# Sliding-window attention with routed experts: the first three routed blocks by seven products, their weight sums on GpSimd, routing dealt out behind every product

## The chip, the cores and the metric

The kernel runs on one core of a Trainium2 chip. The metric is device time in microseconds (us) of one execution, as the median over several runs. Of one execution there is also a hardware profile. In the profile TensorE is PE (its weight loads PEld), VectorE DVE, ScalarE ACT, GpSimd POOL and SyncE SP.

## The reference, cut to what matters

Causal attention with a window of 64 over (8, 8, 576, 64) gives 4608 rows x of 512 numbers. Each row goes through one of 8 experts, all in fp32:

```python
e = argmax(x @ w_gate)          # or the expert of the row before, where x @ w_local says so
p = softmax(x @ w_gate)[e]
out[row] = p * (relu(x[row] @ w1[e]) @ w2[e])   # w1[e]: 512 x 1024, w2[e]: 1024 x 512
```

The expert of a row is taken over from the row before it when a sigmoid gate is at least 0.5, so the choice runs along each sequence of 576 rows as a scan.

## The kernel before

The program has two phases that overlap at their border. **Attention** works through nine groups of 512 rows. Behind it, **routing** finds each row's expert, counts the rows of every expert, and writes tables that say which rows make up each block, with what weight p, and with which expert. It has two halves: the first (`Router.first`) covers the first three sequences and runs within attention; the second (`Router.second`) covers the other rows and runs beside the first three expert blocks. Both are Python generators: after each piece of work they yield the time in us that VectorE is thought to need for it, and whether TensorE's next piece has to wait for it. In `second` the pieces are `gate` (logits to expert, with small transposes on TensorE in between: L801 for vk, L811, L821, L833, and the counting products L845 and L846), then the arithmetic on eight counts per expert, then the places `pl` of the rows (128x296), then `table`: for four pieces of up to ten chunks it builds one-hot matrices `rowh`, `one` and `colh` on VectorE (L934, L939, L944), and TensorE adds up their products (L951). At the end the indices `gx` and `idx` and the weights `pw` are there, and the later blocks' rows can be fetched.

**Experts** work on blocks of 256 rows of one expert (and a few of 128 and 64). The first three, numbered -1, -2 and -3, come from routing's first half (`FB = 3`); thirteen big ones follow, with eight small ones between. A block is `fetch` (two gathers of 128 rows on GpSimd's queue, and two transfers of 2 MB for w1 and w2 on SP's), `turn` (eight transposes on TensorE, two copies into `xt`), `hidden` (relu(x @ w1)) and `result` (h @ w2, times p, with a scatter of each half on GpSimd's queue). Weights land in a ring of four buffers, so w1 of block n+2 is asked for when block n's w1 has been read.

A block is computed in one of two ways. *Plain* (L1275, L1307) uses 32 and 16 full matmuls. *Fast* is the scheme that multiplies 2x2 quarters with seven products in place of eight. It needs sums of the quarters: four of `xt` (128x256 each, tile xs), four of w1 (128x1024, tile ws1), four of w2 (128x1024, ws2) and four of h (128x512, hs). `left` and `right` write them, `prepare` calls those for xt and w1, and `big_hidden` and `big_result` (products at L1184 and L1227 of the kernel before) the others. Each of the sum tiles has one buffer. Between products ScalarE keeps copies of what a PSUM accumulator holds so far, and VectorE adds such a copy to another accumulator (L1195 for h, L1236 for y). Three accumulators px, py and pz are used by turns, so the last product of a half has to wait until the addition that reads px is done.

Blocks -1 and -2 are plain before the change (`PLAIN = (-1, -2)`), block -3 and all later big blocks are fast. While routing's second half runs, only TensorE's order is written out by hand (`manual_schedule(engines={ET.PE})`), and a planner orders VectorE, ScalarE and GpSimd. From block -3 on VectorE and ScalarE are in program order too. TensorE's pieces of routing are dealt out by `step()`, after each group of a plain hidden half and twice per half of a result; each call lowers a pause by `STEP = 3.5`, and a piece is given out when the pause has run down. The whole second half is done before the hidden half of block -3.

Of the kernel before, what the change touches and what calls it, by code (L numbers as in the profile page):

```python
# [8 lines left out]
F32 = mybir.dt.float32  # L9
# [6 lines left out]
ET = mybir.EngineType  # L16
# [3 lines left out]
P = 128  # L20
# [49 lines left out]
MID = (KB, KB - 1)  # L70
PLAIN = (-1, -2)

# [90 lines left out]
def attention(ctx, tc, ring, kq, v3, v4, vt, vh, xs, lt, ok, wg, wg2, ident, rt, ex):  # L163
# [125 lines left out]
    build_mask(0)  # L289
    allr = cp.tile([P, NSC, HP, 2, 4], F32, name="allr")  # L290

# [400 lines left out]
class Router:  # L692
# [306 lines left out]
    def second(self, psum):  # L999
# [16 lines left out]
        rest = tl("rest", P, E)  # L1016
        vec.tensor_tensor(rest, cnt, lim, op=Alu.subtract)
        ns = tl("ns", P, E)
        self.shifted(ns, rest, HF - 1, P.bit_length() - 1)
# [21 lines left out]
        vec.tensor_tensor(steph, hoff, send, op=Alu.subtract)  # L1041
        vec.tensor_scalar(steph, steph, float(P), float((HF0 - SM0) * P), Alu.mult, Alu.add)
        CE = [P, CV, E]
        pl, none = tl("pl", *CE), tl("none", P, C1, E)
# [3 lines left out]
        vec.tensor_tensor(pl, pl, mid(off).to_broadcast(CE), op=Alu.add)  # L1048
        yield 6.0, False
        plh = tl("plh", *CE)  # L1050
# [4 lines left out]
        vec.tensor_tensor(pl[:, :C1], pl[:, :C1], none, op=Alu.add)  # L1055
        vec.tensor_tensor(pl, pl, self.oh, op=Alu.mult)
        lo, hi = self.places(pl, CV)
        ej = tabs["ej"]
        self.experts_of(ej[:, :NBLK], NBLK, [(NB, bend), (E, send), (E, hend)])
# [3 lines left out]
        vec.scalar_tensor_tensor(ej[:, NBLK:], bend[0:1, E - 1:], float(SURE[0]), more, Alu.is_gt, Alu.max)  # L1063
        yield 6.0, False
        at = yield from self.table(psum, slice(0, CV), NS, lo, hi, tabs["idx"], tabs["pw"], tabs["gx"])
# [12 lines left out]
class Experts:  # L1078
# [12 lines left out]
    def rows(self, st, n):  # L1091
        tabs = self.tabs
        if n < 0:
            idx, pw, gx, rows = tabs["idx1"], tabs["pw1"], tabs["gx1"], ZR + 1
            slots = range(-2 - 2 * n, -2 * n)
        else:
            idx, pw, gx, rows = tabs["idx"], tabs["pw"], tabs["gx"], N + 2
            slots = range(2 * n, 2 * n + 2) if n < NB else range(SM0 + n - NB, SM0 + n - NB + 1)
        st.update(x=[], slots=slots, idx=idx, pw=pw, rows=P, big=len(slots) == 2, fast=len(slots) == 2 and n not in PLAIN)
        if n >= NB + E:  # L1100
            st.update(half=n - NB - E, rows=HF)
        for s in slots:
            x = (self.xp if n == -1 else self.xq).tile([P, D], F32, name="xg")
            self.nc.gpsimd.indirect_dma_start(  # L1104
                out=x, out_offset=None, in_=self.xs[:rows, :],
                in_offset=bass.IndirectOffsetOnAxis(ap=gx[:, s:s + 1], axis=0))
            st["x"].append(x)
        return st
# [14 lines left out]
    def turn(self, st, quiet):  # L1123
        nc, n = self.nc, st["rows"]
        st["xt"] = xt = self.xtp.tile([P, DK, BIG], F32, name="xt")
        for i, x in enumerate(st["x"]):
            tp = self.ps_t.tile([P, DK, P], F32, name="tp")
            for kk in range(DK):
                nc.tensor.transpose(tp[:, kk, :n], x[:n, kk * P:(kk + 1) * P], self.ident[:n, :n])  # L1129
            (nc.scalar.copy if quiet else nc.vector.tensor_copy)(xt[:, :, i * P:i * P + n], tp[:, :, :n])  # L1130
        if st["fast"] and not quiet:
            self.prepare(st)

    def prepare(self, st):

        st["xq"] = quarters(st["xt"], DK, BIG)
        st["xt"] = self.right("xs", st["xq"])
        w = quarters(st["w1"], DK, F)

        st["wq"] = [[w[0][0], w[1][0]], [w[0][1], w[1][1]]]  # L1140
        st["ws"] = self.left("ws1", st["wq"])

    def left(self, name, a):

        sub, add = Alu.subtract, Alu.add
        s1, s2, s3, s4 = self.sums(name, a)
        for o, x, y, op in ((s1, a[1][0], a[1][1], add), (s2, s1, a[0][0], sub), (s3, a[0][0], a[1][0], sub),
                            (s4, a[0][1], s2, sub)):
            self.nc.vector.tensor_tensor(o, x, y, op=op)
        return s1, s2, s3, s4  # L1150

    def right(self, name, b):

        sub = Alu.subtract
        t1, t2, t3, t4 = self.sums(name, b)
        for o, x, y in ((t1, b[0][1], b[0][0]), (t2, b[1][1], t1), (t3, b[1][1], b[0][1]), (t4, b[1][0], t2)):
            self.nc.vector.tensor_tensor(o, x, y, op=sub)
        return t1, t2, t3, t4
# [4 lines left out]

    def big_hidden(self, st):

# [7 lines left out]
        st["w2q"] = w2 = quarters(st["w2"], FK, D)  # L1173
        st["w2t"] = self.right("ws2", w2)
        st["h"] = h = self.wk.tile([P, FK, BIG], F32, name="h", bufs=1)
# [22 lines left out]
        product(px, a[0][0], b[0][0], stop=False)  # L1198
        u = keep(0, px)
        product(py, s[0], t[0], stop=False)  # L1200
        z = keep(1, py)
        product(px, s[1], t[1], False, False)
        v = keep(2, px)
        product(pz, a[0][1], b[1][0])
        relu(hq[0][0], pz, u)
        product(px, s[2], t[2], False, False)
        relu(hq[1][1], px, z)
        product(py, s[3], b[1][1], False)
        relu(hq[0][1], py, v)
        product(px, a[1][1], t[3], False)  # L1210
        relu(hq[1][0], px)

        st["ha"] = [[hq[0][0], hq[1][0]], [hq[0][1], hq[1][1]]]
        st["hs"] = self.left("hs", st["ha"])

    def big_result(self, st):

# [20 lines left out]
        product(px, a[0][0], b[0][0], stop=False)  # L1238
        u = keep(0, px, pw[0])
        product(py, s[0], t[0], stop=False)  # L1240
        z = keep(1, py, pw[1])
        product(px, s[1], t[1], False, False)
        v = keep(2, px, pw[0])
        product(pz, a[0][1], b[1][0])
        put(0, 0, pz, u)
        product(px, s[2], t[2], False, False)
        put(1, 1, px, z)
        product(py, s[3], b[1][1], False)
        put(0, 1, py, v)
        self.scatter(st, 0, y[0])  # L1250
        product(px, a[1][1], t[3], False)
        nc.scalar.activation(y[1][:, :w], px, Act.Copy, scale=pw[1])
        self.scatter(st, 1, y[1])

    def scatter(self, st, i, y):
# [5 lines left out]
    def hidden(self, st, quiet, step):  # L1261
        nc = self.nc
        if st["fast"]:
            return self.big_hidden(st)
        n = BIG if st["big"] else st["rows"]
# [17 lines left out]

    def result(self, st, step):
        nc = self.nc
        if st["fast"]:
            return self.big_result(st)
        if "half" in st:
# [27 lines left out]
    def space(self, ctx):  # L1316
        tc = self.tc
        self.xtp = ctx.enter_context(tc.tile_pool(name="ex_xt", bufs=2))
        self.xq = ctx.enter_context(tc.tile_pool(name="ex_xq", bufs=6))
        self.wk = ctx.enter_context(tc.tile_pool(name="ex_work", bufs=2))  # L1320
        self.one = ctx.enter_context(tc.tile_pool(name="ex_one", bufs=1))
        self.ps_t = ctx.enter_context(tc.tile_pool(name="ex_ps_t", bufs=2, space=PSUM))
# [3 lines left out]
    def run(self, ctx, rt, last=None):  # L1326
# [3 lines left out]
        ps_r = ctx.enter_context(tc.tile_pool(name="ex_ps_r", bufs=1, space=PSUM))  # L1330
        ctx.enter_context(tc.manual_schedule(engines={ET.PE}))
        rt.rows_of(ctx, tc, "rt_oh2")
# [5 lines left out]
        side = rt.second(psum)  # L1338
        pause = 0.0

        def step():
            nonlocal side, pause
            pause -= STEP
            if pause > 0.0:
                return
            pause, trip = 0.6, False
            while side and not trip:
                w, trip = next(side, (0.0, None))
# [8 lines left out]
        for n in range(SURE[0]):  # L1357
            order.append(n)
            if n % 2 and between:
                order.append(between.pop(0))  # L1360
        order += between + half[:1]
        jobs += [self.fetch(n) for n in order[1:FB]]
        self.turn(jobs[0], True)
        step()
        for i, n in enumerate(order):
            quiet = i < FB
            if i == FB - 1:
                while side:
                    step()
                if last:  # L1370
                    last(psum())

                ctx.enter_context(tc.manual_schedule(engines={ET.PE, ET.DVE, ET.Activation}))
                jobs.append(self.fetch(order[FB]))
                if jobs[i]["fast"]:
                    self.prepare(jobs[i])
            if i + 2 > FB and i + 2 < len(order):
                jobs.append(self.fetch(order[i + 2]))
            self.hidden(jobs[i], quiet, step)
            if i + 1 < len(order):  # L1380
# [60 lines left out]
```

## Time and profile before

| what | us |
|---|---|
| three runs: median (lowest to highest) | 657.9 (657.87 to 658.69) |
| the profiled execution's own time | 659.1 |
| its span, first to last instruction | 657.1 |
| attention's last matmuls end | 136.4 |
| block -1, hidden half begins (first L1275) | 136.4 |
| block -3, hidden half begins (first L1184) | 202.4 |
| fourth block, hidden half begins | 228.6 |

The span of 657.1 us leaves 2.0 us around it. A row of the timeline has the start in us from the span's start, the duration in us, engine, line, operation, tiles out and in with shapes (partitions x elements), and in brackets the idle time before it with what ended it. A row of a table by stretches has each engine's busy us and its number of instructions (x), the granted TensorE clock as a share of the full one, the share of time that the DMA engines were busy, and GB/s.

### The profile page before, as it was taken

The numbers are of one execution on the slowest core, as the hardware profiler recorded it, in microseconds if no ns is written. First come the engines' busy times: TensorE is split into PE (matmuls) and PEld (weight loads), VectorE is DVE, ScalarE is ACT, GpSimd is POOL, SyncE is SP. The second block draws the span as 40 slices with busy tenths as digits, with TensorE's granted clock in tenths as the row PEclk, the third lists the DMA queues.
The fourth block names the chain that finished last, engine by engine and source line by source line (L and its number), as shares of the span: only waits on it lengthen the run. The fifth ranks groups of instructions, "written<-read, shape, count | busy, mean of one in ns | idle before, by whom it ended". The sixth has DMA issues, their size and how long they took to land. (4 is left out here: it accounts for less than half of the span.)

```text
span 657.1 us, 14909 instructions
## 1 busy us (share of the span) xinstructions
PE 629.8 (96%) x6431; PEld 544.8 (83%) x6431; DVE 401.2 (61%) x723; ACT 181.8 (28%) x314; POOL 125.8 (19%) x131
## 2 busy tenths in 40 slices
PE   7888988899999999999999999999999999999995
PEld 7777767675757999889989998999799979997974
DVE  6675589665984866378628835852765276527310
ACT  4756655421111232112212121221122112211200
POOL 4322122220014111121104113211311130101011
PEclk9999998899999999999999999999999999999999
DMA  8999999895436555595578748746864685457540
GB/s 337 415 346 360 351 377 355 327 378 199 161 144 241 195 212 218 173 397 204 184 278 315 269 180 314 289 169 215 305 240 165 221 309 219 161 213 283 193 157 23
DMA packets 22032, 165.80 MB, mean 252 GB/s; under 512 B 3485, under 2 KB 4515, under 8 KB 11972
## 3 DMA queue, kind: packets, MB, share of 16 engines
q1 hardware_dynamic: 13108, 135.24, 55.4%
q0 software_dynamic: 8848, 29.50, 11.3%
q8 instruction: 53, 0.87, 0.5%
q14 instruction: 23, 0.19, 0.1%
HBM read 145.85 MB, written 19.40 MB: 251 GB/s over the span
## 5 line engine op out<-in xcount | busy, mean ns | idle before, releaser
L1257 POOL DMA_INDIRECT out_dram<-y,idx x36 | 40.9, 1136 | 335.6 <-DVE y L1236 149.2
L1184 PE MATMUL hp<-xs,ws 128*128 128x128 f32 x672 | 79.6, 275 | 0.0
L1184 PEld LDWEIGHTS hp<-xs,ws 128*128 128x128 f32 x672 | 77.3, 192 | 0.0
L1227 PE MATMUL hp<-ws,hs 128*128 128x256 f32 x336 | 77.1, 379 | 0.0
L1275 PE MATMUL hp<-xt,w 128*64 128x64 f32 (+2 forms) x896 | 74.1, 260 | 0.0
L1275 PEld LDWEIGHTS hp<-xt,w 128*64 128x64 f32 (+1 forms) x896 | 68.6, 161 | 5.8 <-issue 2.4
L1227 PEld LDWEIGHTS hp<-ws,hs 128*128 128x128 f32 x336 | 63.8, 190 | 8.7
L1195 DVE TENSOR_TENSOR h<-hp,keep 128x512 f32<-128x512 f32 x42 | 28.8, 690 | 57.3 <-PE hp L1184 57.3
L1104 POOL DMA_INDIRECT xg<-xs,gx x40 | 45.7, 1144 | 72.7 <-PE tp L1129 58.9
L1307 PE MATMUL yp<-w,h 128*128 128x512 f32 x128 | 56.4, 593 | 0.0
L1184 PEld LDWEIGHTS hp<-xt,w 128*128 128x128 f32 x448 | 53.0, 192 | 2.9 <-issue 1.9
L1184 PE MATMUL hp<-xt,w 128*128 128x128 f32 x448 | 54.9, 276 | 0.0
L1236 DVE SCALAR_TENSOR_TENSOR y<-hp,pw,kept 128x256 f32<-128x256 f32 x42 | 19.7, 480 | 57.1 <-issue 33.3
L1227 PE MATMUL hp<-w,h 128*128 128x256 f32 x224 | 53.3, 381 | 0.0
L416 DVE TENSOR_TENSOR p<-p,mask 128x1024 f32<-128x1024 f32 x31 | 38.6, 1244 | 20.6 <-ACT p L411 20.5
L380 PEld LDWEIGHTS sp<-w 64*64 64x64 f32 x1296 | 37.6, 134 | 16.3 <-issue 13.1
L411 ACT ACTIVATE p<-sp 128x512 f32<-128x512 f32 x72 | 39.3, 596 | 40.1 <-PE sp L380 37.9
L426 PE MATMUL xo<-va,p 128*64 128x74 f32 (+1 forms) x576 | 45.7, 233 | 3.3 <-DVE va L343 3.3
L426 PE MATMUL xo<-vb,p 128*64 128x74 f32 (+1 forms) x576 | 45.7, 233 | 3.2 <-ACT p L300 1.5
L380 PE MATMUL sp<-w 64*64 64x128 f32 (+1 forms) x1296 | 43.3, 265 | 5.5 <-issue 4.7
L426 PEld LDWEIGHTS xo<-vb,p 128*64 128x64 f32 x576 | 39.9, 141 | 7.9 <-issue 4.7
L1307 PEld LDWEIGHTS yp<-w,h 128*128 128x128 f32 x128 | 23.7, 190 | 26.9 <-issue 26.1
(257 smaller groups left out, 945.9 us busy)
## 6 DMA issues: line engine op xcount, KB each, us to landing
w<-in_w_dram SPq DMA_DIRECT2D x48, 2048.0 KB, 9.0
w<-in_kq_dram SPq DMA_DIRECT2D x17, 1024.0 KB, 9.4
xs<-x POOLq DMA_DIRECT2D x9, 1024.0 KB
va<-in_v_dram SPq DMA_DIRECT2D x5, 1184.0 KB
vtt<-in_vt_dram SPq DMA_DIRECT2D x5, 1024.0 KB
va<-in_v_dram SPq DMA_DIRECT2D x3, 1040.0 KB, 9.0
va<-in_v_dram SPq DMA_DIRECT2D x2, 520.0 KB, 6.6
w<-in_kq_dram SPq DMA_DIRECT2D x2, 512.0 KB
```

Source lines behind the costliest of these rows:

```text
L380: nc.tensor.matmul(sp[j][c * WIN:(c + 1) * WIN, a:b], lhsT=kt[h, hp, block * WIN:(block + 1) * WIN], rhs=qt[h, hp, a:b], start=not biased, ...
L411: nc.scalar.activation(p[:, j], sp[j], Act.Exp, scale=DH ** -0.5)
L416: masked.append(nc.vector.tensor_tensor(p, p, m.to_broadcast([P, 2, SC]), op=Alu.mult))
L426: nc.tensor.matmul(xo[par * WIN:(par + 1) * WIN, j, s * VW:s * VW + n], lhsT=p[:, j, b * WIN:(b + 1) * WIN], rhs=w[:, s, 2 * hp + j, :n], ...
L1104: self.nc.gpsimd.indirect_dma_start(out=x, out_offset=None, in_=self.xs[:rows, :], in_offset=bass.IndirectOffsetOnAxis(ap=gx[:, s:s + 1], ...
L1184: nc.tensor.matmul(out[:, m, :], lhsT=a[:, kk, m * P:(m + 1) * P], rhs=b[:, kk, :], start=start and m + kk == 0, stop=stop and (m, kk) == ...
L1195: nc.vector.tensor_tensor(o, x, y, op=add)
L1227: nc.tensor.matmul(out, lhsT=a[:, m, :], rhs=b[:, m, :], start=start and m == 0, stop=stop and m == FK // 2 - 1, skip_group_check=True)
L1236: nc.vector.scalar_tensor_tensor(y[i][:, j * w:(j + 1) * w], x, pw[i], y2, Alu.mult, Alu.add)
L1257: self.nc.gpsimd.indirect_dma_start(out=self.out[:, :], out_offset=bass.IndirectOffsetOnAxis(ap=st["idx"][:, s:s + 1], axis=0), in_=y, in_ ...
L1275: nc.tensor.matmul(hp[a, i, :], lhsT=st["w1"][:, kk, m * P:(m + 1) * P][:, a], rhs=st["xt"][:, kk, :n], start=(kk == 0), stop=(kk == DK - 1))
L1307: nc.tensor.matmul(yp, lhsT=st["h"][:, m, i * P:(i + 1) * P], rhs=st["w2"][:, m, :], start=(m == 0), stop=(m == FK - 1))
```

## The change

Blocks -1 and -2 become fast too (`PLAIN` goes, `fast` holds for every big block). For the three early blocks GpSimd writes the sums of w1, and for blocks -1 and -2 also those of w2; the rest stays on VectorE. The copies of xt for the early blocks stay on ScalarE. `step()` is now called after each of the seven products of a half, it lowers the pause by `QUIET = 1.25`, and routing's second half yields in smaller pieces; it may run until the end of block -3's hidden half. While it runs, TensorE, VectorE, ScalarE and GpSimd are all in program order. The flag for the rare path and the fetches of the fourth and fifth block follow after block -3's hidden half, and the fourth block's `turn` is called from inside block -3's result, after four of its seven products. The pool of the sum tiles is opened ahead of the gathered rows' pool, and `allr` moves to another pool.

```diff
-PLAIN = (-1, -2)
+QUIET = 1.25
...
-    allr = cp.tile([P, NSC, HP, 2, 4], F32, name="allr")
+    allr = wk.tile([P, NSC, HP, 2, 4], F32, name="allr", bufs=1)
...
         vec.tensor_tensor(pl, pl, mid(off).to_broadcast(CE), op=Alu.add)
-        yield 6.0, False
+        yield 1.9, False
...
-        if st["fast"] and not quiet:
+        if st["fast"]:
             self.prepare(st)
...
-        st["ws"] = self.left("ws1", st["wq"])
+        st["ws"] = self.left("ws1", st["wq"], self.nc.gpsimd if st["early"] else self.nc.vector)
...
-        st["w2t"] = self.right("ws2", w2)
+        st["w2t"] = self.right("ws2", w2, nc.gpsimd if -FB < st["early"] < 0 else nc.vector)
...
         product(px, a[0][0], b[0][0], stop=False)
         u = keep(0, px)
+        step()
         product(py, s[0], t[0], stop=False)
...
         product(pz, a[0][1], b[1][0])
         put(0, 0, pz, u)
+        step()
+        mid()
         product(px, s[2], t[2], False, False)
         put(1, 1, px, z)
+        step()
...
-        ctx.enter_context(tc.manual_schedule(engines={ET.PE}))
+        early = ExitStack()
+        early.enter_context(tc.manual_schedule(engines={ET.PE, ET.DVE, ET.Activation, ET.Pool}))
...
-        pause = 0.0
+        pause, room = 0.0, QUIET
...
-            pause -= STEP
+            pause -= room
...
-            pause, trip = 0.6, False
-            while side and not trip:
+            trip = False
+            while side and not trip and pause <= 0.0:
...
+        def rest():
+            early.close()
+            ctx.enter_context(tc.manual_schedule(engines={ET.PE, ET.DVE, ET.Activation}))
+            if last:
+                last(psum())
+            jobs.extend(self.fetch(n) for n in order[FB:FB + 2])
+        self.turn(jobs[0], True)
         jobs += [self.fetch(n) for n in order[1:FB]]
         for i, n in enumerate(order):
+            if i + 2 >= FB + 2 and i + 2 < len(order):
+                jobs.append(self.fetch(order[i + 2]))
+            self.hidden(jobs[i], i < FB, step)
             if i == FB - 1:
                 while side:
                     step()
+                rest()
+                self.result(jobs[i], step, lambda: self.turn(jobs[FB], False))
+                continue
```

More of the change, by code (lines that the diff above doesn't have):

```diff
@@ L1017, in second @@
         vec.tensor_tensor(rest, cnt, lim, op=Alu.subtract)
+        yield 1.6, False
         ns = tl("ns", P, E)
@@ L1042, in second @@
         vec.tensor_scalar(steph, steph, float(P), float((HF0 - SM0) * P), Alu.mult, Alu.add)
+        yield 1.6, False
         CE = [P, CV, E]
@@ L1056, in second @@
         vec.tensor_tensor(pl, pl, self.oh, op=Alu.mult)
+        yield 2.4, False
         lo, hi = self.places(pl, CV)
+        yield 2.2, False
         ej = tabs["ej"]
@@ L1063, in second @@
         vec.scalar_tensor_tensor(ej[:, NBLK:], bend[0:1, E - 1:], float(SURE[0]), more, Alu.is_gt, Alu.max)
-        yield 6.0, False
+        yield 1.2, False
         at = yield from self.table(psum, slice(0, CV), NS, lo, hi, tabs["idx"], tabs["pw"], tabs["gx"])
@@ L1098, in rows @@
             slots = range(2 * n, 2 * n + 2) if n < NB else range(SM0 + n - NB, SM0 + n - NB + 1)
-        st.update(x=[], slots=slots, idx=idx, pw=pw, rows=P, big=len(slots) == 2, fast=len(slots) == 2 and n not in PLAIN)
+        st.update(x=[], slots=slots, idx=idx, pw=pw, rows=P, big=len(slots) == 2, fast=len(slots) == 2, early=n if n < 0 else 0)
         if n >= NB + E:
@@ L1136, in prepare, with left @@
         st["xq"] = quarters(st["xt"], DK, BIG)
-        st["xt"] = self.right("xs", st["xq"])
+        st["xt"] = self.right("xs", st["xq"], self.nc.vector)
         w = quarters(st["w1"], DK, F)
         st["wq"] = [[w[0][0], w[1][0]], [w[0][1], w[1][1]]]
-        st["ws"] = self.left("ws1", st["wq"])
-    def left(self, name, a):
+        st["ws"] = self.left("ws1", st["wq"], self.nc.gpsimd if st["early"] else self.nc.vector)
+    def left(self, name, a, engine):
         sub, add = Alu.subtract, Alu.add
@@ L1148, in left, with right @@
                             (s4, a[0][1], s2, sub)):
-            self.nc.vector.tensor_tensor(o, x, y, op=op)
+            engine.tensor_tensor(o, x, y, op=op)
         return s1, s2, s3, s4
-    def right(self, name, b):
+    def right(self, name, b, engine):
         sub = Alu.subtract
@@ L1156, in right @@
         for o, x, y in ((t1, b[0][1], b[0][0]), (t2, b[1][1], t1), (t3, b[1][1], b[0][1]), (t4, b[1][0], t2)):
-            self.nc.vector.tensor_tensor(o, x, y, op=sub)
+            engine.tensor_tensor(o, x, y, op=sub)
         return t1, t2, t3, t4
@@ L1162, in sums, with big_hidden @@
         return [t[:, i] for i in range(4)]
-    def big_hidden(self, st):
+    def big_hidden(self, st, step):
         nc, add = self.nc, Alu.add
@@ L1199, in big_hidden @@
         u = keep(0, px)
+        step()
         product(py, s[0], t[0], stop=False)
         z = keep(1, py)
+        step()
         product(px, s[1], t[1], False, False)
         v = keep(2, px)
+        step()
         product(pz, a[0][1], b[1][0])
         relu(hq[0][0], pz, u)
+        step()
         product(px, s[2], t[2], False, False)
         relu(hq[1][1], px, z)
+        step()
         product(py, s[3], b[1][1], False)
         relu(hq[0][1], py, v)
+        step()
         product(px, a[1][1], t[3], False)
@@ L1213, in big_hidden, with big_result @@
         st["ha"] = [[hq[0][0], hq[1][0]], [hq[0][1], hq[1][1]]]
-        st["hs"] = self.left("hs", st["ha"])
-    def big_result(self, st):
+        st["hs"] = self.left("hs", st["ha"], nc.vector)
+        step()
+    def big_result(self, st, step, mid):
         nc = self.nc
@@ L1239, in big_result @@
         u = keep(0, px, pw[0])
+        step()
         product(py, s[0], t[0], stop=False)
         z = keep(1, py, pw[1])
+        step()
         product(px, s[1], t[1], False, False)
         v = keep(2, px, pw[0])
+        step()
         product(pz, a[0][1], b[1][0])
         put(0, 0, pz, u)
+        step()
+        mid()
         product(px, s[2], t[2], False, False)
         put(1, 1, px, z)
+        step()
         product(py, s[3], b[1][1], False)
@@ L1250, in big_result @@
         self.scatter(st, 0, y[0])
+        step()
         product(px, a[1][1], t[3], False)
@@ L1253, in big_result @@
         self.scatter(st, 1, y[1])
+        step()
     def scatter(self, st, i, y):
@@ L1263, in hidden @@
         if st["fast"]:
-            return self.big_hidden(st)
+            return self.big_hidden(st, step)
         n = BIG if st["big"] else st["rows"]
@@ L1282, in hidden, with result @@
             step()
-    def result(self, st, step):
+    def result(self, st, step, mid=lambda: None):
         nc = self.nc
         if st["fast"]:
-            return self.big_result(st)
+            return self.big_result(st, step, mid)
         if "half" in st:
@@ L1318, in space @@
         self.xtp = ctx.enter_context(tc.tile_pool(name="ex_xt", bufs=2))
+        self.one = ctx.enter_context(tc.tile_pool(name="ex_one", bufs=1))
         self.xq = ctx.enter_context(tc.tile_pool(name="ex_xq", bufs=6))
         self.wk = ctx.enter_context(tc.tile_pool(name="ex_work", bufs=2))
-        self.one = ctx.enter_context(tc.tile_pool(name="ex_one", bufs=1))
         self.ps_t = ctx.enter_context(tc.tile_pool(name="ex_ps_t", bufs=2, space=PSUM))
@@ L1361, in run @@
         order += between + half[:1]
+        def rest():
[5 more added lines that the diff above has]
+        self.turn(jobs[0], True)
         jobs += [self.fetch(n) for n in order[1:FB]]
-        self.turn(jobs[0], True)
-        step()
         for i, n in enumerate(order):
-            quiet = i < FB
+            if i + 2 >= FB + 2 and i + 2 < len(order):
+                jobs.append(self.fetch(order[i + 2]))
+            self.hidden(jobs[i], i < FB, step)
             if i == FB - 1:
@@ L1369, in run @@
                     step()
[L1370 to L1379, printed above, removed]
+                rest()
+                self.result(jobs[i], step, lambda: self.turn(jobs[FB], False))
+                continue
             if i + 1 < len(order):
```

## The prediction

> **What bounds the kernel now.** I read the page's busy table and slices first, then the stretch that the change rewrites, engine by engine.
>
> ```profile
> PE 629.8 (96%) x6431; PEld 544.8 (83%) x6431; DVE 401.2 (61%) x723; ACT 181.8 (28%) x314; POOL 125.8 (19%) x131
> ...
> PE   7888988899999999999999999999999999999995
> ```
>
> TensorE is the bound: from about 130 us on, every slice has it at 90% or more. The chain of waits covers only the last 16 us of stores and says nothing about the middle. So a change is worth what it takes from TensorE's queue, less any wait that it puts there. The stretches of the three early blocks (first block's hidden and half its result; up to the end of block two; block three), by engine:
>
> ```profile
> core 0: us, PE busy (x) PEld busy (x) DVE busy (x) ACT busy (x) POOL busy (x), PEclk, DMA share, GB/s
> 136.40:168.10 31.70, 30.53 (x119) 19.92 (x116) 18.73 (x86) 4.51 (x8) 5.77 (x6) 1.00 0.66 259
> 168.10:202.40 34.30, 32.98 (x143) 22.49 (x142) 30.75 (x34) 5.42 (x9) 4.29 (x3) 1.00 0.45 158
> 202.40:228.80 26.40, 26.05 (x180) 24.41 (x180) 14.88 (x35) 5.60 (x10) 8.93 (x9) 1.00 0.65 233
> ```
>
> GpSimd's column is nearly empty, and VectorE's second row is 30.75 of 34.30: routing's second half has VectorE almost to itself there, and not much room is left. TensorE's timeline of the same stretch has the prices of both kinds of block:
>
> ```profile
> 136.43 3.72 PE L1275 MATMUL hp<-xt,w 128*128 128x256 f32 x16
> 141.33 0.38 PE L801 MATMUL r<-ident,vk 128*23 128x128 f32 x2 [1.17 <-DVE vk L794]
> ...
> 168.09 13.98 PE L1275 MATMUL hp<-xt,w 128*128 128x256 f32 x64
> 181.90 1.04 PE L1129 MATMUL tp<-ident,xg 128*128 128x128 f32 x8
> ...
> 202.31 0.27 PE L156 MATMUL r<-ident,ok 128*1 128x128 f32 x1 [1.31 <-DVE t L953]
> 202.42 2.02 PE L1184 MATMUL hp<-xt,w 128*128 128x128 f32 x16
> ...
> 213.72 2.05 PE L1184 MATMUL hp<-xs,w 128*128 128x128 f32 x16 [0.35 <-DVE h L1195]
> ```
>
> A plain hidden half takes 168.09 to 181.90 = 13.8 us, a plain result the same (four stretches of 8 matmuls at 3.45 us). Seven products start 1.78 us apart in the hidden half (12.5 us) and 1.725 us apart in the result (12.1 us). TensorE's only waits are 1.17, 1.31 and 0.35 us.
>
> **What the Trainium skill says.** Three places bear on this. "GPSIMD Engine Reference", 3.1 Elementwise, gives a GpSimd tensor_tensor add of 2048 fp32 per partition as 4497 ns; the trace before has no such operation, so 2.25 us for 1024 is an estimate from that page (VectorE takes 1.22 us for it, rows of L1149). "SBUF — State Buffer", Who interferes with whom: "A DVE instruction with two SBUF inputs contends with a GpSimd instruction that reads SBUF", and whoever starts second is held until the first ends. The trace agrees. GpSimd and VectorE early in attention:
>
> ```profile
> 17.99 1.04 POOL L356 COPY vb<-va 64x1040 f32<-64x1040 f32 x1 [3.52 <-DMA va<-in_v_dram]
> 18.98 2.05 POOL L360 COPY vb<-va 64x1040 f32<-64x1040 f32 x1
> ...
> 18.52 1.59 DVE L416 TENSOR_TENSOR p<-p,mask 128x1024 f32<-128x1024 f32 x1 [0.65 <-ACT p L411]
> 20.04 0.20 DVE L431 RECIPROCAL allr<-xo 128x8 f32<-128x8 f32 x1
> ...
> 98.24 1.28 POOL L360 COPY vb<-va 64x1184 f32<-64x1184 f32 x1
> ...
> 98.52 1.13 DVE L989 SCALAR_TENSOR_TENSOR pl<-pl,rank 128x112 f32<-128x112 f32 x1
> ```
>
> The mask product (1.22 us elsewhere) is held until the copy ends at 19.03, and the next copy (1.04 us) until the product ends at 20.11. At 98.52 an operation of some 0.27 us lasts 1.13: it ends just after the copy (98.24 + 1.28 = 99.52). The two take turns, one instruction each, so a tiny VectorE operation can cost a whole GpSimd one. An operation with one input in PSUM (L436) is not held. "TensorE: Matmul & The Clock Gate", Part 1, says that an idle window of about 3.4 us halves the clock; after the idle time at 98.2 (3.3 us) the trace has PEclk 0.50 from 101.3 to 104.6.
>
> **The change, part by part.**
>
> *Removed from TensorE.* Two plain blocks become seven products: 2 x (13.8 - 12.5) + 2 x (13.8 - 12.1) = 6.0 us. The waits 1.17 + 1.31 + 0.35 = 2.8 us go from their places: -8.8 us in all, if nothing new waits.
>
> *Added to VectorE.* For each of two blocks: sums of xt 4 x 0.42, of h 4 x 0.69, three h additions of 0.69, three y additions of 0.48: 7.9 us, 15.9 us for both. The first-weight sums of block three leave (4 x 1.22 = 4.9). Net +11.0.
>
> *Added to GpSimd.* 20 sums (three blocks' w1, two blocks' w2) x 2.25 = 45 us where 19 us was busy in 92. Queued behind them: the last xs store, the four gathers of blocks two and three (1.3 us each to issue; they go out some 8 us later and still land ahead of block two's turn, which the waits below push back more), the scatters. The weights' transfers on SP now also wait for GpSimd (the ring's buffers are read by its sums); with 8.1 to 8.5 us from issue to landing and a block of over 25 us, that stays hidden. ScalarE takes 7 small copies more per block, at 5 us busy in 30: hidden. The pools' new places: I cost them at nothing, since the first sum waits for attention's last product either way (its buffer lies where p was). The moved weight and row fetches hide behind block three's result.
>
> *The two together.* Nearly all routing operations and the sums of xt and h have two SBUF inputs. So GpSimd's 45 us and VectorE's work stand in one line. I walked the queues of the four engines in the program's own order from 136.4, with the durations of the rows above, 2.25 us for a GpSimd sum, one turn each. TensorE's new waits, in order:
>
> - block one, product two, for the first GpSimd sum and the xt sum held behind it: 1.1
> - the transposes of vk, queued behind product two: VectorE is held by sums two, three and four (3 x 2.2) and does 1.7 of xt sums first: 7.9
> - the counting products, whose onehot is held by a w2 sum: 3.0
> - result, product two, needs hs; eight GpSimd sums run back to back and five tiny operations (base, cnt, start) each pay one (5 x 2.2, less what TensorE is still doing): 8.1
> - the last product reuses px, and the addition that reads it stands behind some 40 routing operations on VectorE: 5.4
> - block two's result, for w2 sums that could begin only when block one's last product released their buffer: 2.5 + 1.0
> - the table's first 20 matmuls, for colh: rowh, hs, xt sums and colh are held by four w1 sums of block three: 8.2
> - px again, block two: 1.1
> - block three: the next block's turn now stands amid the result, and its copies (1.3), xt sums (1.7) and w1 sums (4.9) are ahead of the addition that frees px; two products (3.45) cover part: 4.2
>
> Sum 42.5 us. 42.5 - 8.8 = **+33.7 us**. After block three the order is as before, so it is carried to the end. The profiled execution took 659.1 us (span 657.1 and 2.0 around it), 1.2 above the runs' median 657.9: 692.8 on its own footing, **691.6 us** for the median.
>
> *Unknowns.* The GpSimd sum: below, a copy of 1040 through its port is 1.04 us, so two inputs are about 2.05 us, and 1.8 would take unusual overlap; above, 2.5. The walk moves by 19 us per us: 683 at 1.8, 696 at 2.5. The clock: four or five waits above 5 us may each bring 3.4 us at half clock; since VectorE and GpSimd then set the pace, 0 to 8 us; I take 0, since much of it falls into other waits. Holding could be weaker for long sums than for copies: down to the next case.
>
> **Rivals.** *No holding.* If GpSimd's sums leave VectorE alone, the same walk has 0.5 + 1.7 + 5.3 + 1.1 + 4.2 = 12.8 us of waits: +4.0, 662 us. For: the page's price was taken alone. Against: the two examples above.
>
> *Faster.* The mechanism is room: routing's deadline moves from the end of block two to the end of block three's hidden half, 12.5 us later, while VectorE gets only 11.0 us more. If it isn't held, and its additions are reached in time in block one, only the turn amid block three (4.2) and the first sum (0.5) wait: 4.7 - 8.8 = -4.1, 653.8 us. It decides from the point where all new waits stay under 8.8 us, that is, if at most 4 us remain of the first two blocks' waits. Against: the 40 operations ahead of the px addition don't need GpSimd to be late.
>
> *Worse.* Sums of 2.5 us and the clock together: 691.6 + 5 + 8 = 705 us, and more if stores and gathers issue slower beside the sums.
>
> **How the numbers follow.** Held: 0.76, its own range 676 to 704. No holding: 0.12, nearly all slower. Faster: 0.07. Worse: 0.05. A measurement of this kernel tells 0.2% (1.3 us) from no change. Faster by more: 0.08 (with a tail of no holding). Within: 0.03. Slower: 0.89. For 8 in 10, 662 to 708 takes in the held case and the middle of no holding.
>
> **What would show it.** In the profile after: GpSimd sums of 128x1024 at 2 us or more, back to back; VectorE's small routing operations at 1 to 2 us beside them, and not elsewhere; TensorE at 6 or 7 tenths for the slices from 136 to 260, with waits named vk, colh and hs; block three's result waiting some 4 us for y. A gap of some 125 us from the first early product to the fourth block's (92.1 now) shows the sum right. Wrong: routing operations at their old durations beside GpSimd's sums, or waits together under 9 us.

## The result, and the profile after

| | us |
|---|---|
| before, median of four runs (lowest to highest) | 657.9 (657.2 to 658.7) |
| after, median of four runs (lowest to highest) | 699.0 (696.9 to 701.6) |
| ratio, 95% interval | 1.063 (1.059 to 1.066) |
| after, the profiled execution's own time, and its span | 696.9, 694.9 |

The change made the kernel 41 us slower by the medians; the forecast was 34 slower. (The two profiled executions lie 37.8 apart, 659.1 and 696.9: that of after is the lowest of its four.) The page's busy table and slices of after, to lay beside those of before:

```profile
PE 635.9 (92%) x6575; PEld 562.7 (81%) x6575; DVE 446.4 (64%) x747; ACT 186.1 (27%) x324; POOL 180.1 (26%) x151
...
PE   8899888846884998999999999999999999999996
...
PEclk9999999978897999999999999999999999999998
```

TensorE is at 4 to 8 tenths in the five slices from 139 to 226 us (the ninth digit on), where it had been at 90% or more. It also has 6 us more of busy time, though the change took 6 us of products from it, and the clock row shows why: 7, 8, 8, 9 and 7 tenths in these slices. The three early blocks by stretches (block one; two; three):

```profile
core 0: us, PE busy (x) PEld busy (x) DVE busy (x) ACT busy (x) POOL busy (x), PEclk, DMA share, GB/s
133.90:189.35 55.45, 34.76 (x190) 30.65 (x187) 51.16 (x112) 6.88 (x13) 34.45 (x18) 0.82 0.47 176
189.35:233.16 43.81, 31.49 (x197) 27.45 (x196) 36.16 (x27) 7.11 (x13) 25.98 (x10) 0.88 0.22 75
233.16:266.16 33.00, 28.84 (x196) 26.31 (x194) 22.36 (x40) 6.14 (x11) 10.82 (x11) 0.97 0.73 256
```

VectorE's column carries it: 51.16 of 55.45 us in block one, where busy time holds the standing behind GpSimd as well as the work. From here on I call the time from the first early product to the first product of the fourth block *the stage*. It was 228.57 - 136.43 = 92.1 us; it is 266.16 - 133.92 = 132.2 us, 40.1 more. What lies behind it is the same in both: 657.1 - 228.6 = 428.5 us, and 694.9 - 266.2 = 428.7. Its start moves from one execution to the next: in after it came 2.5 us sooner than in before, and in e4_mid_later below, whose program is the same as after's up to there, it came at 139.3. So the stages are compared, and not the spans. TensorE's timeline of after, where it waits and right behind it:

```profile
147.97 0.62 PE L801 MATMUL r<-ident,vk 128*23 128x128 f32 x2 [9.08 <-DVE vk L794]
...
162.26 0.98 PE L845 MATMUL r<-oh,ones 128*128 128x184 f32 x2 [2.81 <-DVE oh L839]
...
172.43 5.14 PE L1238 MATMUL hp<-ws,hs 128*128 128x256 f32 x16 [3.52 <-DVE hs L1153]
...
186.14 3.38 PE L1238 MATMUL hp<-ws,h 128*128 128x256 f32 x8 [3.39 <-DVE y L1247]
...
220.78 2.41 PE L951 MATMUL r<-colh,rowh 128*128 128x270 bf16 x10 [8.06 <-DVE colh L944]
222.97 3.62 PE L1238 MATMUL hp<-w,h 128*128 128x256 f32 x8
...
263.32 3.04 PE L1238 MATMUL hp<-ws,h 128*128 128x256 f32 x8 [4.16 <-DVE y L1247]
```

The brackets are the waits. The durations behind them are the clock: eight matmuls of 128x256 last 1.9 us elsewhere, and 3.4 to 3.6 in the fourth and sixth row; the two counting products of the second row last 0.98, where they lasted 0.47 before. The granted clock from 161.8 to 165.0 us is 0.50. Why VectorE is late is seen by laying its timeline beside GpSimd's:

```profile
152.35 2.36 POOL L1161 TENSOR_TENSOR ws<-w,ws 128x1024 f32<-128x1024 f32 x1
154.67 2.35 POOL L1161 TENSOR_TENSOR ws<-w 128x1024 f32<-128x1024 f32 x1
...
166.57 2.48 POOL L1153 TENSOR_TENSOR ws<-w,ws 128x1024 f32<-128x1024 f32 x1
...
153.05 1.71 DVE L817 TENSOR_TENSOR_SCAN carry<-crow 1x23 f32<-1x23 f32 x1
154.88 0.69 DVE L1199 TENSOR_TENSOR h<-hp,keep 128x512 f32<-128x512 f32 x1
...
166.86 2.59 DVE L853 TENSOR_TENSOR_SCAN run<-te,zero 128x184 f32<-128x184 f32 x1
...
169.86 0.17 DVE L859 TENSOR_TENSOR cnt<-run,base 128x8 f32<-128x8 f32 x1
```

A scan over 23 numbers begins in the middle of a GpSimd sum and ends at 154.76, just behind the sum's end at 154.71. The h addition after it, with an input in PSUM, takes its usual 0.69 in the midst of the next sum. The scan L853 (0.54 elsewhere) waits for the last sum, which ends at 169.05; from then on small operations last 0.17 again.

### The profile page after: what moved, and what is told of

Its sections match the earlier page's. It is cut to its first block, busy times and chain, and to the rows that moved or that the text cites. A ratio compares the mean times of both kernels' runs of the same rounds, so it can differ in the third digit from the quotient of the medians.

```text
span 694.9 us, 15295 instructions
## 1 busy us (share of the span) xinstructions
PE 635.9 (92%) x6575; PEld 562.7 (81%) x6575; DVE 446.4 (64%) x747; ACT 186.1 (27%) x324; POOL 180.1 (26%) x151
## 5 line engine op out<-in xcount | busy, mean ns | idle before, releaser
L1238 PE MATMUL hp<-ws,hs 128*128 128x256 f32 x384 | 90.0, 384 | 6.5 <-DVE hs L1153 6.5
L1188 PE MATMUL hp<-xs,ws 128*128 128x128 f32 x768 | 93.0, 278 | 0.9 <-POOL ws L1153 0.9
L1188 PEld LDWEIGHTS hp<-xs,ws 128*128 128x128 f32 x768 | 90.1, 195 | 1.1 <-POOL ws L1153 1.1
L1238 PEld LDWEIGHTS hp<-ws,hs 128*128 128x128 f32 x384 | 73.9, 193 | 17.9 <-issue 3.9
L1238 PE MATMUL hp<-w,h 128*128 128x256 f32 x256 | 62.5, 388 | 0.0
L1238 PEld LDWEIGHTS hp<-w,h 128*128 128x128 f32 x256 | 48.4, 195 | 6.4
L1200 ACT ACTIVATE h<-h 128x512 f32<-128x512 f32 x48 | 30.2, 630 | 72.1 <-DVE h L1199 68.9
L1294 PEld LDWEIGHTS hp<-xt,w 128*64 128x64 f32 (+1 forms) x768 | 44.5, 156 | 2.0 <-issue 1.8
L1194 ACT COPY keep<-hp 128x512 f32<-128x512 f32 x48 | 28.1, 586 | 65.3 <-PE hp L1188 65.3
L1294 PE MATMUL hp<-xt,w 128*64 128x64 f32 (+1 forms) x768 | 45.0, 240 | 0.0
```

The lines of the kernel that those rows point to most:

```text
L1188: nc.tensor.matmul(out[:, m, :], lhsT=a[:, kk, m * P:(m + 1) * P], rhs=b[:, kk, :], start=start and m + kk == 0, stop=stop and (m, kk) == ...
L1194: nc.scalar.copy(o, x)
L1200: nc.scalar.activation(o, x if y is None else o, Act.Relu)
L1238: nc.tensor.matmul(out, lhsT=a[:, m, :], rhs=b[:, m, :], start=start and m == 0, stop=stop and m == FK // 2 - 1, skip_group_check=True)
L1294: nc.tensor.matmul(hp[a, i, :], lhsT=st["w1"][:, kk, m * P:(m + 1) * P][:, a], rhs=st["xt"][:, kk, :n], start=(kk == 0), stop=(kk == DK - 1))
```

## The experiments

All are made from after unless it says otherwise. The ratio is to runs of before made beside each (medians 657.5 to 659.1). "Stage" is from the one profile of each, less the 92.1 of before's one profile.

| kernel | median us | ratio to before (95%) | stage us, less 92.1 |
|---|---|---|---|
| after | 699.0 | 1.063 (1.059 to 1.066) | +40.1 |
| e1_pool_fill | 673.3 | 1.022 (1.017 to 1.027) | +13.1 |
| e2_dve_sums | 689.4 | 1.047 (1.043 to 1.052) | +31.7 |
| e3_dealing | 673.1 | 1.022 (1.018 to 1.026) | +15.1 |
| e4_mid_later | 692.8 | 1.052 (1.048 to 1.056) | +33.2 |
| e5_warm | 695.6 | 1.057 (1.054 to 1.059) | +38.1 |
| e6_unused_sums | 691.1 | 1.051 (1.047 to 1.055) | +33.0 |
| e7_paced | 655.5 | 0.995 (0.993 to 0.997) | -2.8 |
| e8_half_fast | 656.6 | 0.998 (0.997 to 0.9995) | -1.5 |
| e9_chained_sums | 689.5 | 1.048 (1.045 to 1.052) | +30.6 |
| e10_ordered | 688.9 | 1.048 (1.044 to 1.052) | +30.3 |
| e11_fill_ordered | 662.1 | 1.006 (1.004 to 1.009) | +1.5 |
| e12_same_sums | 691.1 | 1.048 (1.045 to 1.051) | +33.2 |

The theory to test was the forecast's: GpSimd's sums hold VectorE, and the wait ends at TensorE. Its rivals were that VectorE's work is late whether held or not (its order, its load), and that the clock does it.

**e1_pool_fill: GpSimd as busy, but reading nothing.**

```diff
-            engine.tensor_tensor(o, x, y, op=op)
+            self.sum(engine, o, x, y, op)
...
+    def sum(self, engine, o, x, y, op):
+        if engine is self.nc.gpsimd:
+            engine.memset(o, 0.0)
+            engine.memset(o, 1.0)
+        else:
+            engine.tensor_tensor(o, x, y, op=op)
```

> After, with each of GpSimd's twenty early weight sums replaced by two fills of the same 128x1024 tile with a constant (the sums themselves are left out; GpSimd has about as much to do, some 2.0 to 2.2 us per sum going by the 0.53 us of the fill of 520 columns, but reads nothing of SBUF). Turn-taking: VectorE is no longer held, its routing operations are back at their durations of before, and only the waits of the no-holding case are left: 662 us, up to 666 with some half clock. Rival, lateness: VectorE's longer programme and GpSimd's busy time alone are the cause, whether or not anything is held: over 685 us. Rival, any GpSimd work holds VectorE, reading or not: 690 us or more, and routing operations of 1 to 2 us beside the fills.

673.3 us: the stage loses 27.0 of its 40.1 us. So two thirds of the loss hang on GpSimd reading SBUF. A pair of fills is some 0.4 us shorter than a sum (2 x 0.95 against 2.35), but TensorE waits for GpSimd itself only at the first sum, 0.16 us here and 0.86 in after, so this explains little. VectorE's timeline beside the fills (0.95 us each, the last of them here ends at 165.8; L1169 is the line of all sums on VectorE in this kernel):

```profile
159.36 0.69 DVE L1169 TENSOR_TENSOR hs<-hs,h 128x512 f32<-128x512 f32 x1
...
163.92 0.88 DVE L884 TENSOR_SCALAR sh_i<-sh_i 128x8 int32<-128x8 int32 x1
164.83 0.97 DVE L885 CAST nb<-sh_i 128x8 f32<-128x8 int32 x1
...
168.08 0.17 DVE L884 TENSOR_SCALAR sh_i<-sh_i 128x8 int32<-128x8 int32 x1
```

Sums of two SBUF tiles (L1169) are not held by a fill, while casts and TENSOR_SCALAR operations are: 0.88 and 0.97 beside the fills, 0.17 after them. That is how the Trainium skill has it ("SBUF — State Buffer", Who interferes with whom: a two-input operation contends with GpSimd's reads only, a copy, cast or tensor_scalar in a two-port mode with any use of the shared pair). The forecast had used only the first half of it. The 662 to 666 us expected were missed by 7 us or more. The stage says where: 15.9 us of waits against 12.8, above all one of 7.10 for the addition that frees px (5.3 forecast), and 5.8 us more of TensorE's own time, most of it half clock (busy for 89.4 us against 89.6 - 6.0). TensorE's timeline:

```profile
175.44 3.59 PE L1245 MATMUL hp<-ws,h 128*128 128x256 f32 x8 [7.10 <-DVE y L1254]
```

**e2_dve_sums: the sums on VectorE.**

```diff
-        st["ws"] = self.left("ws1", st["wq"], self.nc.gpsimd if st["early"] else self.nc.vector)
+        st["ws"] = self.left("ws1", st["wq"], self.nc.vector)
...
-        st["w2t"] = self.right("ws2", w2, nc.gpsimd if -FB < st["early"] < 0 else nc.vector)
+        st["w2t"] = self.right("ws2", w2, nc.vector)
```

> After, with the twenty early weight sums on VectorE in place of GpSimd (1.22 us each, 24.4 us more for VectorE, nothing for GpSimd). Turn-taking: nothing is held, but VectorE itself is now the longer queue of the stage, 75 to 80 us of work of after plus 24: 681 us without half clock, 689 with it, so 10 to 18 us better than after and still well over before. Rival, GpSimd's sums cost VectorE nothing: then 24.4 us of new work on the engine that is late make it slower than after, 705 us or more.

689.4, as the theory had it: the engine that is late gets 24 us more of work, and the kernel is 10 us faster than after. GpSimd's help cost VectorE more than doing the sums itself.

**e3_dealing: the dealing without the products.**

```diff
-        st.update(x=[], slots=slots, idx=idx, pw=pw, rows=P, big=len(slots) == 2, fast=len(slots) == 2, early=n if n < 0 else 0)
+        st.update(x=[], slots=slots, idx=idx, pw=pw, rows=P, big=len(slots) == 2, fast=len(slots) == 2 and n not in (-1, -2), early=n if n < 0 else 0)
...
-        st["ws"] = self.left("ws1", st["wq"], self.nc.gpsimd if st["early"] else self.nc.vector)
+        st["ws"] = self.left("ws1", st["wq"], self.nc.vector)
```

> After, with blocks one and two by plain products again (as in before) and block three's first-weight sums on VectorE: only the new dealing of routing's second half behind every product, the order written out for more engines and the turn amid block three's result are left of the change. If the sums and the seven products cause the loss, this stands near before; walking the queues gives +11 us from the turn amid the result, the additions behind routing's pieces and the later table, so 669 us, up to 672 with half clock. If the dealing is the cause of most of the loss: 685 us or more. If it costs nothing: 658 us.

673.1, a little over the 669 to 672. With plain blocks the dealing differs from after's, since there are fewer calls of `step()`; VectorE stands idle from 173.1 to 181.7 us with the table's pieces not yet given out, and TensorE then waits 7.63 and 1.22 for colh, and 4.16 in block three's result:

```profile
217.21 2.41 PE L951 MATMUL r<-colh,rowh 128*128 128x270 bf16 x10 [7.63 <-DVE colh L944]
```

So the dealing and the turn cost 15 us at this pace even with plain blocks and nothing on GpSimd.

**e4_mid_later: block three's turn.**

```diff
         step()
-        mid()
         product(px, s[2], t[2], False, False)
         put(1, 1, px, z)
+        mid()
```

> After, with the next block's turn amid block three's result called one product later, behind the addition that frees px. The 4.16 us wait for y in block three's result should go: 695 us (4 us better than after's 699), at most 6 better. Rival: the wait only moves to the next block's first product, since its sums of xt and weights come later: 698 to 700 us.

692.8, 6.2 better, a little more than the most expected; the wait of 4.16 us is gone and nothing takes its place. In after the last product behind that wait ran at 3.04 us for 1.9, and the fourth block's first at 2.60 for 1.95: the rest of the 6.

**e5_warm: TensorE kept busy while it waits.**

```diff
+        if part:
+            self.warm(22)
         tp = psum()[:n, :2 * P].rearrange("c (i p) -> c i p", i=2)
...
+    def warm(self, n):
+        yp = self.ps_y.tile([P, D], F32, name="yp")
+        for _ in range(n):
+            self.nc.tensor.matmul(yp[:, :CMAX * E], lhsT=self.ident, rhs=self.still, start=True, stop=True)
```

> After, with matmuls of constants (128x184, into a bank of PSUM that nobody reads) put in TensorE's queue just ahead of the places where it waits: 22 ahead of the transposes of vk, 5 ahead of the counting products, 8 and 8 ahead of block one's result product two and last product, 3 and 2 in block two's, 19 ahead of the second group of the table's matmuls, 11 ahead of block three's last product; each group is a little shorter than the wait measured there. The waits for VectorE get shorter by what the constants fill, and TensorE doesn't fall to half clock. Theory one, half clock is a loss of its own: the products of after's stage are back at full speed and all of their excess (about 11 us) goes: 688 us. Theory two, most of it is absorbed, since VectorE and GpSimd set the pace between the waits: 3 to 6 us better than after, 693 to 696 us. Rival, the clock has no part in it: 699 us or more.

695.6: theory two. In the stage the constants take 78 x 0.32 = 25 us and the waits left are 16.6, together 41.6 where after waited 37.0. The stage of 130.3 us leaves 130.3 - 92.1 + 8.8 - 41.6 = 5.4 us of excess in TensorE's own work, where the same sum gives 11.9 in after. So 6.5 us of it went, and 4.6 came back as time without products: one wait for hs is still 4.08 us long, behind eight constants. Half clock is real, but most of it lies where VectorE is late anyway. The gain is small beside the scatter (2.0 us in the stage, 3.4 in the medians; the two intervals still touch).

**e6_unused_sums, e9_chained_sums, e12_same_sums: holding by itself.** These are made from before. GpSimd gets sixteen sums that nobody uses. The three differ in what the sums are: independent, each reading the last, and the very ones of after.

```diff
+        if quiet and not st["fast"]:
+            for name, q in (("ws1", quarters(st["w1"], DK, F)), ("ws2", quarters(st["w2"], FK, D))):
+                o = self.sums(name, q)
+                for i in range(4):
+                    nc.gpsimd.tensor_tensor(o[i], q[i // 2][i % 2], q[1][1 - i % 2], op=Alu.add)
```

> Before, with sixteen sums of 128x1024 on GpSimd that nothing uses (four of w1 and four of w2 for each of the two plain blocks, written to the tiles that the seven products use later). VectorE gets no new work and TensorE's queue is as before. Turn-taking: VectorE's routing operations last 1 to 2.6 us beside the sums, the table comes late, and TensorE waits for vk, colh and the table's tail: +18 to +21 us, so 676 to 679 us. Rival, no holding: GpSimd was idle there, so nothing moves but the store and gathers queued behind the sums: 658 to 660 us.

691.1: holding alone, with no work added to VectorE and nothing changed in TensorE's queue, costs 33 us; no wait that the trace names in the stage is for a gather or a transfer. It is far more than the 18 to 21 that turns would cost, and the timelines of VectorE, GpSimd and TensorE of that run say why:

```profile
149.53 0.19 DVE L814 COPY crow<-r 1x46 f32<-1x46 f32 x1 [4.11 <-PE r L812]
149.76 29.65 DVE L817 TENSOR_TENSOR_SCAN carry<-crow 1x23 f32<-1x23 f32 x1
...
147.15 32.21 POOL L1137 TENSOR_TENSOR ws<-w 128x1024 f32<-128x1024 f32 x14
...
179.56 0.17 PE L821 MATMUL r<-ident,carry 1*23 1x1 f32 x1 [26.42 <-DVE carry L817]
```

One scan over 23 numbers was held from the second of fourteen sums to the end of the last (147.15 + 32.21 = 179.36). VectorE didn't get a turn at any of the boundaries. TensorE waited 26.42 us for it. I asked whether a sum that depends on the one before lets VectorE in, and then whether after's own sums do:

```diff
-                    nc.gpsimd.tensor_tensor(o[i], q[i // 2][i % 2], q[1][1 - i % 2], op=Alu.add)
+                    nc.gpsimd.tensor_tensor(o[i], o[i - 1] if i else q[0][0], q[i // 2][i % 2], op=Alu.add)
```

> e6_unused_sums with each group's four sums chained: every sum but the first reads the one before it, as after's second and fourth sums do, so GpSimd's next sum has to wait for the end of the last one. In e6_unused_sums a scan of 1x23 elements was held for 29.65 us, over some thirteen sums in a row that depend on nothing, and not for one. Theory, VectorE gets in where GpSimd's stream has to wait: here it waits at most sums, the two take turns, and the loss is what was forecast for turn-taking: 676 to 680 us, no routing operation over some 5 us. Rival, a run of sums holds VectorE to its end whatever their dependence: 690 us again, and again an operation of 20 us or more.

```diff
-                o = self.sums(name, q)
-                for i in range(4):
-                    nc.gpsimd.tensor_tensor(o[i], q[i // 2][i % 2], q[1][1 - i % 2], op=Alu.add)
+            w = quarters(st["w1"], DK, F)
+            self.left("ws1", [[w[0][0], w[1][0]], [w[0][1], w[1][1]]], nc.gpsimd)
+            self.right("ws2", quarters(st["w2"], FK, D), nc.gpsimd)
```

(`left` and `right` get the engine as an argument, as in after.)

> e6_unused_sums with the very sums that after does for blocks one and two (the same operands and operations, add and subtract by turns of the quarters of w1 and w2), unused, in the order of before. In after a VectorE operation got in at nearly every boundary between two GpSimd sums; in e6_unused_sums and e9_chained_sums a scan of 1x23 was held over about thirteen of them. Theory one, what the sums are (operands, operations) decides: here VectorE gets in as in after, and the time is what was forecast for turn-taking, 676 to 680 us. Theory two, a run of sums may hold VectorE to its end whichever sums they are, and what VectorE and the others do at the boundary decides: an operation of 20 us or more again, 688 to 691 us.

Neither: 689.5 and 691.1, with the same scan at 28.73 us in e9_chained_sums and, in VectorE's timeline of e12_same_sums:

```profile
148.03 29.89 DVE L817 TENSOR_TENSOR_SCAN carry<-crow 1x23 f32<-1x23 f32 x1
```

So what the sums are doesn't decide. Their order isn't quite tested, since the planner orders GpSimd in these three: in e12_same_sums it puts sums of w1 and w2 by turns (L1153 at 145.66, L1161 at 147.96, L1153 at 150.27), and in e9_chained_sums it starts both chains ahead of what reads them, so a sum need not stand right behind the one that it reads. But in after the same instruction got in at the first boundary (1.71 us above), and the sum that began there, at 154.67, reads only w and nothing of the sum before it. So GpSimd's having to wait for its last sum isn't needed to let VectorE in. What lets it in there and not here stays open.

**e7_paced and e8_half_fast: what is left when nothing is held.** The first is e3_dealing with

```diff
-QUIET = 1.25
+QUIET = 1.8
...
         step()
-        mid()
         product(px, s[2], t[2], False, False)
         put(1, 1, px, z)
+        mid()
```

> e3_dealing with two edits: the amount that a step gives out is 1.8 in place of 1.25, and the next block's turn amid block three's result is called one product later, behind the addition that frees px. If e3_dealing's loss is its pace (routing's table pieces given out behind block three's turn and sums) and that turn, and not the dealing as such, all of it goes, and with it the waits that before has for vk and the table's tail: 2 to 3 us better than before, 655 us. Rival: dealing and the order written out cost something whatever their pace: 662 us or more.

The second, made from after, has only block two's hidden half by seven products, with the same later turn and all sums on VectorE. `FH` and `FR` list the early blocks whose hidden half and whose result are fast, the empty `G1` and `G2` those with sums on GpSimd:

```diff
-QUIET = 1.25
+QUIET = 1.5
+FH, FR, G1, G2 = (-2, -3), (-3,), (), ()
...
-        if st["fast"]:
+        if st["fastr"]:
             return self.big_result(st, step, mid)
```

> The smallest part of the change that still takes products from TensorE: only the hidden half of block two by seven products (1.3 us less for TensorE), its weight sums on VectorE, block one and block two's result plain, a step giving out 1.5 and the turn as in e7_paced. VectorE gets 1.7 + 4.9 + 2.1 us more before routing must be done. If room on VectorE is what decides, this is about the most that fits: the new waits (1.1 for the counting products, 2.1 for the table, 1.4 for rows of block four) eat the gain: 658 to 659 us, 2 to 3 us behind e7_paced. Rival: seven products still pay where no sum is on GpSimd: 654 us or less.

e7_paced is the fastest kernel here: 655.5, 0.5% under before, by what was expected. TensorE's one wait of the stage is this one:

```profile
208.21 0.98 PE L951 MATMUL r<-colh,rowh 128*128 128x270 bf16 x7 [0.52 <-DVE colh L944]
```

So dealing behind every group and the written order are worth having; e3_dealing lost by its pace and by the turn, which were changed together here (e4_mid_later has the turn alone at some 6 us, made from after). e8_half_fast is at 656.6, better than the 658 to 659 expected, with waits of 0.35, 1.40 and 0.87 us. It is 1.1 us behind e7_paced: the 1.3 us of products saved are less than the 2.1 us more of waits. Its pace differs too (1.5 against 1.8), so this says that this part of the seven products didn't pay at the pace tried, and not that it can't.

**e10_ordered and e11_fill_ordered: the additions that free px first.** The edit is the same on after and on e1_pool_fill:

```diff
         u = keep(0, px, pw[0])
-        step()
         product(py, s[0], t[0], stop=False)
         z = keep(1, py, pw[1])
-        step()
         product(px, s[1], t[1], False, False)
         v = keep(2, px, pw[0])
-        step()
         product(pz, a[0][1], b[1][0])
         put(0, 0, pz, u)
-        step()
-        mid()
         product(px, s[2], t[2], False, False)
         put(1, 1, px, z)
-        step()
+        mid()
+        for _ in range(5):
+            step()
```

> After with nothing in VectorE's queue ahead of the additions that free px: routing's pieces are given out in the fast result halves only once that addition stands in the queue (five steps at once after it), and the next block's turn in block three one product later. GpSimd's sums stay. The waits for y (3.4, 1.3 and 4.2 us) should go, some of the table's wait should grow: 689 to 692 us. Rival, order on VectorE was the main cost: 680 us or less.

> The same edit on e1_pool_fill (fills of a constant in place of GpSimd's early sums, whose values are left out). With no holding and no wait for y, only some 1 to 3 us of waits are left for the first fill, vk and block two's hidden half, against 6.0 us of products saved and before's 2.8 us of waits: 656 to 659 us, about the time of before. That is then what the seven products of two more blocks are worth at the very most. Rival, some cost of the change is not yet named: 665 us or more.

e10_ordered came to 688.9, as expected: all waits for y are gone, the one for colh falls to 5.72, and a new one of 5.22 for h stands in block two. Order was worth 10 us, holding was not touched. e11_fill_ordered came to 662.1 where 656 to 659 was expected. Its stage is 1.5 us above before's, with 8.9 us of waits, the longest 3.54 for h in block two. The profiled execution, at 659.1, was the lowest of its eight runs, 3 us under the median. The record names two differences: its stage began at 133.3 us, 3.2 sooner than before's, and its granted clock over the whole execution was 0.995, where the seven others had 0.985 to 0.991. How much each is worth isn't shown. With sums that cost VectorE next to nothing and hardly a wait for px, seven products in two more blocks don't beat before at the pace of 1.25. With a pace like e7_paced's they were not tried.

## Why the prediction was right, and where it was off

The side, the bound and the mechanism were right; 699.0 lies 7.4 above the 691.6 and within 662 to 708. Part of the closeness is luck: the waits came out 5.5 us smaller than forecast and TensorE's own time 11.9 larger, which partly cancel. Step by step, in the stage's own terms: 37.0 of new waits - 2.8 of old ones - 6.0 of products + 11.9 = 40.1. The last term is what is left over. Some 10 us of it is half clock, counted from the start of each slow product to the start of what follows; the rest is mostly the ends of products ahead of the waits, some 0.2 us each, which overlap with the next product where none waits. It is also seen in the tables by stretches: TensorE was busy for 89.6 us before and is for 95.1 after, where 83.6 were due, so 11.5.

- **Products removed, 6.0 us.** Right. At full clock the products follow each other at the spacing that was assumed (1.78 us from 238.7 to 245.9, 1.73 from 247.8 to 252.9 in the timeline of after).
- **GpSimd's sum, 2.25 us.** 2.35 to 2.39 as a rule, and 2.64 to 2.79 (once 3.60) where it takes turns with VectorE's sums of xt and h. By the walk's 19 us per us, some 2 us too little.
- **The new waits, 42.5 us.** 37.0. In their order, forecast and measured: first sum 1.1 and 0.9; vk 7.9 and 9.1; counting products 3.0 and 2.8 (with 0.9 on small transposes ahead of them); hs 8.1 and 3.5; y in block one 5.4 and 3.4; block two's result 3.5 and 3.0; colh 8.2 and 8.1; y in block two 1.1 and 1.3; y in block three 4.2 and 4.2. The size of hs is the one that failed: the five tiny operations on the counts were to pay a sum each, but GpSimd's run had ended at 169.05, when VectorE had come only to L853, and they took 0.17 to 0.35 us each. Block two's result waits were put down to late w2 sums; the profile names hs, whose four sums last 2.72 to 2.83 each beside GpSimd's sums for block three.
- **The clock, 0 of "0 to 8".** This is the term that was mis-sized: some 10 of the 11.9 us. Only waits above 5 us were reckoned with, but waits of 9.1, 2.8, 3.5, 3.4, 8.1 and 4.2 us were each followed by products at half speed. The argument that much of it falls into other waits was right in the main: e5_warm won back 3.4 us, not 12, so 11.9 in the ledger is not what the kernel would gain without it.
- **"The two take turns, one instruction each".** Right as the picture of after in most places. It isn't a rule: an xt sum begun at 139.73 lasted 5.47 us, through two GpSimd sums, and e6_unused_sums, e9_chained_sums and e12_same_sums have a run of some thirteen that let nothing in. The walk came near since in after VectorE mostly got its turns; as nothing here shows what decides that, it was luck.
- **The rivals.** "No holding" was to give 662; e1_pool_fill gave 673, for the reasons above. The 662 of e11_fill_ordered isn't that case come true, since its order takes out waits for y that the 662 had counted in. "Faster" was to need all new waits under 8.8 us: e11_fill_ordered reached 8.9 without any reading on GpSimd, and wasn't faster.
- **Costed at nothing.** Transfers of weights, gathers, scatters and the pools' new places name no wait in TensorE's timeline of the stage. That holds.

## What to carry to other kernels

Before giving an idle GpSimd two-input work, look at what VectorE does at the same time: here twenty sums of some 2.4 us on GpSimd cost the stage 27 us more than fills that read nothing, and with VectorE doing them itself the kernel was 10 us faster. Where TensorE is the bound and VectorE's queue feeds it, an accumulator's last reader belongs ahead of the work that isn't urgent; that order, a later turn of block four included, was worth 10 us. And a deal of small pieces is worth what its pace and its place make of it: with another pace and a later turn the same dealing gave 655 us in place of 673.

## What was not expected of the hardware

- A run of GpSimd sums can hold one VectorE instruction over all of them: 28.7 to 29.9 us for a scan of 0.19 us, in each of the three kernels built to see it.
- Beside fills, which read nothing, casts and TENSOR_SCALAR operations of VectorE lasted up to 0.97 us in place of 0.17, and two-input sums of 128x512 no longer than elsewhere (0.69).
- A wait of 2.81 us, shorter than those for which the forecast had allowed half clock, was followed by a granted TensorE clock of 0.50 (161.8 to 165.0 us in after).
- GpSimd's sum of 128x1024 takes 2.30 us (32.21 / 14), and a fill of the same tile 0.95.
